# Second expert product on four 32-column tiles of TensorE at once, with rows scattered per round

## The chip, the core and the metric

The kernel runs on one core of a Trainium2 chip. The metric is the device time of one execution in microseconds (us), taken as the median over runs. The profile is of one execution; its span, 296.2 us, is what its engines and queues show, and is about 3 us shorter than the device time of the same runs.

The engines are named as in the profile: PE is TensorE, which multiplies matrices (PEld is its loading of weights, the stationary operand), DVE is VectorE, ACT is ScalarE, POOL is GpSimd, SP is the engine that only issues transfers.

## The reference, cut to what matters

An attention over 4 x 8 heads of 768 positions with 64 dimensions, in which each query attends to 6 chosen chunks of 32 keys, gives 3072 rows (tokens) of 512 numbers. These rows then go to one of 8 experts each:

```python
logits = x @ w_gate                      # 3072 x 8
expert_idx = np.argmax(logits, axis=1)   # one expert a token
gate_w = probs[np.arange(N), expert_idx]
out = np.zeros((N, D))
for e in range(8):
    tok_idx = np.where(expert_idx == e)[0]
    # the 80 tokens with the largest gate_w stay, the others give rows of zeros
    h = np.maximum(x[tok_idx] @ w1[e], 0.0)         # 80x512 @ 512x1024
    out[tok_idx] = gate_w[tok_idx, None] * (h @ w2[e])   # 80x1024 @ 1024x512
```

The change concerns the last product alone, `h @ w2[e]`, with its factor and its way to `out`.

## The kernel before

The work has two parts. The first, up to about 246 us, is the attention: 16 steps, one for each pair of heads of a batch, each with scores, softmax and values, and in between the routing of the batch that went before (which token goes to which expert, and which 80 stay). The rows of x are written to a buffer in device memory, `x_rows`, pair by pair; zeros are written to `out` early; the weights w1 and w2 of all experts are loaded during the attention, so that they lie in SBUF when the second part begins.

The end of the routing belongs to the last batch and can overlap with nothing: gates, ranks, a table. `rank_count` counts, `rank_hot` makes a one-hot matrix OHS, `table` (L750) sums the tokens' numbers and gate values by slot on PE, and `merge` puts them together with the earlier batches on DVE. The result is, for each of 80 slots (partitions) and 8 experts, the row number `idx` (L766) and the gate value `gT` (L770). `dT` holds what the row numbers are made from.

Then comes the expert stage, in which there is an order written out by hand. For an expert e:

- `gather(e)` (L958, POOL): an indirect transfer of 80 rows from `x_rows`.
- `turn(e)` (L967): four PE transposes, and an ACT copy (L970) to `xT`, two buffers.
- `up(e)` (L978): 32 matmuls of 80 columns, x @ w1, in two halves in PSUM. The ReLU of the first half is done by ACT (L985), that of the second half by DVE (L987); both write `hT`, two buffers, 8 blocks of 80 columns.
- `down(e)` (L1009): 8 matmuls, one for each 128 of the 1024 hidden dimensions. The stationary operand is 128 x 80 of `hT`, the moving one 128 x 512 of w2. The result is 80 x 512 in a PSUM bank (OB, two banks). DVE multiplies it by the gate value (L1013), POOL issues an indirect scatter of 80 rows of 2 KB (L1015) to `out`.
- `down_halves` takes the place of `down` for expert 7: the same in two halves of 256 columns (L994, L997, L999), so that the first half is scaled while the second is computed.

Each engine works through its instructions in the order in which they are written. On PE the order is turn(e+1), up(e), down(e-1): the product of expert e-1 runs while the ReLU of expert e is computed. `keep_warm(9)` (L814) gives PE nine matmuls without use ahead of turn(0), while the first gather is under way. A helper, `op`, gives each operation its waits from the names of what it reads and writes.

Instructions that write 32 partitions of PSUM occur in the attention already: `sums_lg` (L569) and `sums` (L583) put four matmuls with 32-column weights side by side, each to its own 32 partitions, and so does `rank_count` (L727).

Of the kernel before, what the change touches and what calls it, by code (L numbers as in the profile page):

```python
# [4 lines left out]
ALU = mybir.AluOpType  # L5
ACTF = mybir.ActivationFunctionType
# [3 lines left out]
U32 = mybir.dt.uint32  # L10
# [137 lines left out]
def bass_quest_chunk_select__then__topk_capacity_drop_kernel(  # L148
# [55 lines left out]
    with ExitStack() as pers:  # L204
# [3 lines left out]
        def al(stack, nm, shape, dt=F32, psum=False):  # L208
            cnt[0] += 1
            f = nc.psum_tensor if psum else nc.sbuf_tensor  # L210
            return stack.enter_context(f(nm + "_" + str(cnt[0]), list(shape), dt))
# [10 lines left out]
        with nc.Block() as blk:  # L222

            @blk.sync
            def _body(_unused):
# [68 lines left out]
                mk = al(pers, "mk", [CAP, E], U32)  # L294
                rk8 = al(pers, "rk8", [CAP, E])
                idx = al(pers, "idx", [CAP, E], U32)


                def Cs(b, jt, n, lo, w):
# [36 lines left out]
                    return bass.AP(rq, (e % 2) * 160, [[S, 128], [1, 160]]).bitcast(BF16)  # L336

                def hTv(e):
                    return bass.AP(qT[e % 2], 0, [[S, 128], [1, FB * CAP // 2]]).bitcast(BF16)

                def yv(e):
                    return bass.AP(EXB, 2048 + (e % 4) * 512, [[EXP, CAP], [1, Dm]])

                def yk(e):
                    return f"y{e % 4}"

                MBf = bass.AP(MB, 0, [[1024, 128], [1, 1024]]).bitcast(F32)
                ubm = bass.AP(M0, 192, [[512, 128], [160, 2], [32, NT - 1], [1, 32]])
# [270 lines left out]
                def scale_rows(i):  # L619
                    b, p = i // NPB, i % NPB  # L620
                    xi = bass.AP(OB, 0, [[1024, 128], [128, NT], [D, 2], [1, D]])
                    xo = bass.AP(xp, 0, [[NT * 128, 128], [128, NT], [D, 2], [1, D]])
                    rx = bass.AP(rden, 0, [[NT * 2, 128], [2, NT], [1, 2], [0, D]])
                    op("dve", lambda: ve.tensor_tensor(xo, xi, rx, ALU.mult), r=["O0", "O1", "rden"], w=["xp"])  # L624
                    xdst = bass.AP(xd.tensor, xd.offset + b * S * Dm + p * 128, [[Dm, 128], [128 * Dm, NT], [1, 128]])
                    op("sp", lambda: sp.dma_start(xdst, xp[:]), r=["xp"], w=[f"xd{i}"],
                       dsem=f"d_xd")
# [126 lines left out]
                def merge(b):  # L754
                    tv = M0[0:CAP, 0:5 * E].rearrange("p (a b) -> p a b", a=5)
                    if b == 0:
                        op("dve", lambda: ve.tensor_copy(dT[:], tv), r=["M0"], w=["dT"])
                        gsum(gT[:], dT, ["dT"], "gT")
                        return
                    nd = 2 if b == B - 1 else 5  # L760
                    gsum(gN[:], tv, ["M0"], "gN")
                    op("dve", lambda: ve.tensor_tensor(mk[:], gN[:], gT[:], ALU.is_gt), r=["gN", "gT"], w=["mk"])
                    mb = bass.AP(mk, 0, [[E, CAP], [0, nd], [1, E]])
                    op("dve", lambda: ve.copy_predicated(dT[:, 0:nd, :], mb, tv[:, 0:nd, :]), r=["mk", "M0", "dT"], w=["dT"])
                    if b == B - 1:
                        op("dve", lambda: ve.scalar_tensor_tensor(idx[:], dT[:, 0, :], 8192.0, dT[:, 1, :], ALU.subtract, ALU.subtract,  # L766
                                                                  reverse0=True), r=["dT"], w=["idx"])
                    else:
                        op("dve", lambda: ve.tensor_copy(dTb[:], dT[:]), r=["dT"], w=["dTb"])
                    op("dve", lambda: ve.copy_predicated(gT[:], mk[:], gN[:]), r=["mk", "gN", "gT"], w=["gT"])  # L770

                def sort_rows(split):
                    for e in range(E):
# [162 lines left out]
                rank_row(b)  # L936
                rank_pred()
                gate_cols(b)
                scale_rows(NP - 1)
                gate_digits(b)  # L940
                last_cmp(5)
# [5 lines left out]
                rank_count(b, (5, 4, 1, 3, 2, 0))  # L947
                rank_slot(b)
                rank_hot(b)
                table(b)  # L950
                merge(b)


                XD = [f"xd{i}" for i in range(NP)]
# [17 lines left out]
                def up(e):  # L972
                    s = e % 2
                    for hf in range(2):
                        for fb in range(hf * 4, hf * 4 + 4):
                            for d in range(DB):
                                o = SC[s][:, hf * 512 + (fb % 4) * CAP:hf * 512 + (fb % 4 + 1) * CAP]
                                op("pe", lambda: pe.matmul(o, w1s[e][:, d, ts(fb)], xTv(e)[:, d * CAP:(d + 1) * CAP],  # L978
                                                           start=(d == 0), stop=(d == DB - 1)),
                                   r=[f"w1_{e}", f"xT{s}"], w=[f"H{s}{hf}", f"SC{s}"], inc=(fb % 4 == 3 and d == DB - 1))  # L980
                        src = SC[s][:, hf * 512:hf * 512 + 4 * CAP]
                        dst = hTv(e)[:, hf * 4 * CAP:(hf + 1) * 4 * CAP]
                        k0 = [f"qT{s}"] if e < 2 and hf == 0 else []
                        if hf == 0:
                            op("act", lambda: ac.activation(dst, src, ACTF.Relu), r=[f"H{s}{hf}"], w=[f"hT{s}{hf}"] + k0)  # L985
                        else:
                            op("dve", lambda: ve.tensor_scalar(dst, src, 0.0, None, ALU.max), r=[f"H{s}{hf}"], w=[f"hT{s}{hf}"])  # L987

                def down_halves(e):
                    s = e % 2  # L990
                    for hf, o, k in ((0, OB[0:CAP, s * 512:s * 512 + Dm // 2], f"O{s}"), (1, SC[1 - s][0:CAP, 0:Dm // 2], f"SC{1 - s}")):
                        cs = slice(hf * Dm // 2, (hf + 1) * Dm // 2)
                        for fb in range(FB):
                            op("pe", lambda: pe.matmul(o, hTv(e)[:, fb * CAP:(fb + 1) * CAP], w2v(e)[:, fb, cs],  # L994
                                                       start=(fb == 0), stop=(fb == FB - 1)),
                               r=[f"hT{s}{fb // 4}"] + w2k(e), w=[k], inc=(fb == FB - 1))
                        op("dve", lambda: ve.tensor_scalar(yv(e)[:, cs], o, gT[:, e:e + 1], None, ALU.mult),  # L997
                           r=[k, "gT"], w=[yk(e)])
                    op("gpd", lambda: gp.indirect_dma_start(  # L999
                        out, bass.IndirectOffsetOnAxis(ap=idx[:, e:e + 1], axis=0), yv(e), None,  # L1000
                        bounds_check=NTOK - 1, oob_is_err=False), r=[yk(e), "idx"] + [f"outz{g}" for g in range(B)], w=[f"out{e}"], dsem=f"d_o{e % 4}")

                def down(e):
                    s = e % 2
                    if e == E - 1:
                        return down_halves(e)
                    o = OB[0:CAP, s * 512:s * 512 + Dm]
                    for fb in range(FB):
                        op("pe", lambda: pe.matmul(o, hTv(e)[:, fb * CAP:(fb + 1) * CAP], w2v(e)[:, fb, :],  # L1009
                                                   start=(fb == 0), stop=(fb == FB - 1)),  # L1010
                           r=[f"hT{s}{fb // 4}"] + w2k(e), w=[f"O{s}"], inc=(fb == FB - 1))
                    k0 = ["E2", "E3", "E4", "E5"] if e == 0 else []
                    op("dve", lambda: ve.tensor_scalar(yv(e), o, gT[:, e:e + 1], None, ALU.mult),  # L1013
                       r=[f"O{s}", "gT"], w=[yk(e)] + k0)
                    op("gpd", lambda: gp.indirect_dma_start(  # L1015
                        out, bass.IndirectOffsetOnAxis(ap=idx[:, e:e + 1], axis=0), yv(e), None,
                        bounds_check=NTOK - 1, oob_is_err=False), r=[yk(e), "idx"] + [f"outz{g}" for g in range(B)], w=[f"out{e}"], dsem=f"d_o{e % 4}")

                for e in range(3):
                    gather(e)  # L1020
                keep_warm(9)
                turn(0)
                gather(3)
# [3 lines left out]
                for e in range(1, E):  # L1027
                    if 1 < e + 1 < E:
                        turn(e + 1)
                        if e + 4 < E:  # L1030
                            gather(e + 4)
                    up(e)
                    down(e - 1)
                down(E - 1)
                sy.wait_for("sp", [f"d_o{m}" for m in range(4)])

        sy.close()
# [33 lines left out]
```

## Time and profile before

| what | value |
|---|---|
| device time, median of 3 runs | 299.59 us (299.08 to 306.82) |
| span of the profiled execution | 296.2 us |
| PE busy | 277.8 us (94%) |
| DVE, ACT, POOL busy | 208.8, 145.0, 233.8 us |
| first matmul of turn(0) | 262.89 us |
| start of up(0), up(1), down(0) | 263.74, 266.58, 268.20 us |
| last matmuls of expert 7 end at about | 290.7 us |
| last scatter begins on POOL | 292.04 us |
| matmuls of L1009 | 56, of 379 ns |
| matmuls of L994 | 16, of 272 ns |
| indirect transfers on POOL | 16, of about 0.93 us each, 2.6 us to landing |

A matmul's recorded time is from its start to the modelled end of its last result; matmuls overlap, so that the distance from one start to the next is shorter than the record. Times in the profile count from the start of the span. A "granted clock" of 1.00 is TensorE at full speed.

### The profile page before, as it was taken

The page shows a single profiled execution, that of the slowest core. Times are in us where ns is not written, and L with a number is a line of the kernel's source. Part 1 is how long each engine was busy: PE and PEld are TensorE (multiplying, and loading weights), DVE is VectorE, ACT ScalarE, POOL GpSimd, SP SyncE. Part 2 cuts the span into 40 slices and gives each one's busy share as a digit, 9 for nine tenths or more (in the row PEclk, how much of TensorE's full clock was granted, in tenths as well). Part 3 has the DMA queues.
Part 4 walks back from the last instruction along what each step waited for, and adds up shares of the span by engine and source line. Part 5 has one row for each costly group of instructions (what it writes and reads, how often), then busy time and mean ns, then how long its engine had stood idle before and what let it go on. Part 6 is the DMA issues. An engine that isn't in the chain of part 4 may idle for free.

```text
span 296.2 us, 8268 instructions
## 1 busy us (share of the span) xinstructions
PE 277.8 (94%) x3400; PEld 171.9 (58%) x3402; DVE 208.8 (70%) x561; ACT 145.0 (49%) x197; POOL 233.8 (79%) x299
## 2 busy tenths in 40 slices
PE   7679999999999999999999999999999999579992
PEld 7245565655656565656565657565646566247662
DVE  3867282746797989659889898898897886803332
ACT  2155646565657555545764546566654541512210
POOL 5049999989898999989899999898999993055332
PEclk9779999999999999999999999999999999879999
DMA  9998999998999999999999999899438299511212
GB/s 150 172 156 135 294 190 138 291 229 154 165 159 197 183 164 186 182 187 169 165 186 177 168 174 214 133 192 361 169 69 158 21 175 191 99 41 47 61 45 66
DMA packets 155141, 47.52 MB, mean 160 GB/s; under 512 B 139128, under 2 KB 147444, under 8 KB 155104
## 3 DMA queue, kind: packets, MB, share of 16 engines
q1 hardware_dynamic: 138528, 27.95, 47.9%
q0 software_dynamic: 13440, 18.67, 38.7%
q10 hardware_dynamic: 3136, 0.39, 0.9%
q8 instruction: 26, 0.43, 0.6%
q14 instruction: 11, 0.09, 0.1%
HBM read 53.10 MB, written 10.75 MB: 216 GB/s over the span
## 4 chain that ended last, share of the span: by engine, by line
PE 67%; POOL 16%; DVE 6%; DMA 6%; issue 2%; ACTq 1%; POOLq 0%; ACT 0%; DVEq 0%
PE SC L510 21%; PE OB L560 18%; POOL ES L549 12%; PE SC L525 4%; PE OB L1009 4%; DMA x_rows<-xp 4%; PE SC L978 4%; PE M L583 4%; PE OB L604 3%; POOL EXB L540 3%; PE M L473 2%; PE M L569 2%; PE MB L498 2%; DMA kn<-in_k_dram 1%; DMA qn<-x_rows,idx 1%
## 5 line engine op out<-in xcount | busy, mean ns | idle before, releaser
L530 ACT ACTIVATE EXB<-SC 128x1024 f32<-128x1024 f32 x96 | 86.2, 916 | 49.2 <-PE SC L525 47.9
L549 POOL TENSOR_TENSOR ES<-ES,EXB 128x256 f32<-128x256 f32 (+1 forms) x108 | 105.7, 991 | 4.9
L510 PE MATMUL SC<-qT,kT 64*128 64x512 f32 (+3 forms) x512 | 99.5, 479 | 1.0 <-ACT EXB L530 1.0
L560 PE MATMUL OB<-EXB,vn 128*64 128x256 f32 (+2 forms) x704 | 72.3, 360 | 0.4 <-POOL EXB L540 0.4
L560 PEld LDWEIGHTS OB<-EXB,vn 128*64 128x64 f32 x704 | 47.0, 137 | 23.6 <-issue 9.0
L510 PEld LDWEIGHTS SC<-qT,kT 64*128 64x128 f32 x512 | 42.6, 191 | 25.0 <-issue 15.1
L549 POOL TENSOR_TENSOR ES<-EXB 128x768 f32<-128x768 f32 (+1 forms) x32 | 49.9, 1558 | 2.7
L525 PE MATMUL SC<-unsT,ind 64*128 64x128 bf16 (+5 forms) x256 | 38.3, 294 | 0.8 <-ACT unsT L500 0.8
L564 ACT ACTIVATE oT<-OB 128x512 f32<-128x512 f32 (+1 forms) x32 | 15.6, 489 | 44.3 <-PE OB L560 44.3
L540 POOL TENSOR_SCALAR_AFFINE_SELECT EXB<-EXB 128x256 f32<-128x256 f32 x80 | 35.1, 448 | 0.0
L525 PEld LDWEIGHTS SC<-unsT,ind 64*128 64x128 bf16 x256 | 13.0, 96 | 18.3 <-issue 8.0
L574 DVE STREAM_TRANSPOSE M<-M 128x192 f32<-128x192 f32 x16 | 6.3, 394 | 23.1 <-PE M L583 21.2
L441 DVE STREAM_TRANSPOSE qT<-qn 128x768 f32<-128x768 f32 x16 | 15.6, 972 | 9.4 <-PE SC L525 9.4
L624 DVE TENSOR_TENSOR xp<-OB,rden 128x768 bf16<-128x768 f32 x16 | 15.3, 955 | 7.0 <-PE OB L604 6.1
L445 ACT ACTIVATE rq<-qT 128x768 f32<-128x768 f32 x16 | 13.5, 843 | 9.7 <-DVE qT L441 8.9
L451 DVE STREAM_TRANSPOSE kT<-kn 128x768 f32<-128x768 f32 x16 | 15.5, 967 | 3.6 <-DMA kn<-in_k_dram 3.5
L1015 POOL DMA_INDIRECT out_dram<-EXB,idx x7 | 6.5, 931 | 12.8 <-DVE EXB L1013 7.8
L958 POOL DMA_INDIRECT qn<-x_rows,idx x4 | 3.9, 982 | 15.7 <-DVE gT L770 13.2
L455 DVE TENSOR_REDUCE kmm<-kT 128x24 f32<-128x768 f32 x16 | 15.2, 950 | 0.5
L457 POOL TENSOR_TENSOR kmm<-kmx,kmm 128x24 f32<-128x24 f32 x16 | 7.3, 454 | 10.4 <-DVE wg L833 6.8
L456 DVE TENSOR_REDUCE kmx<-kT 128x24 f32<-128x768 f32 x16 | 15.1, 943 | 0.0
L487 DVE MAX8 top<-M 128x8 f32<-128x8 f32 (+4 forms) x160 | 14.6, 166 | 0.6
(163 smaller groups left out, 404.7 us busy)
## 6 DMA issues: line engine op xcount, KB each, us to landing
w1s<-in_moe_w_dram POOLq DMA_DIRECT2D x8, 1024.0 KB, 9.2
w2s<-in_moe_w_dram POOLq DMA_DIRECT2D x7, 1024.0 KB, 10.6
qn<-in_q_dram SPq DMA_DIRECT2D x64, 96.0 KB, 3.3
vn<-in_v_dram SPq DMA_DIRECT2D x32, 192.0 KB, 3.5
out_dram<-w1s SPq DMA_DIRECT2D x4, 1536.0 KB, 9.1
kn<-in_k_dram SPq DMA_DIRECT2D x60, 96.0 KB, 3.2
x_rows<-xp SPq DMA_DIRECT2D x16, 192.0 KB, 4.7
EXB<-in_moe_w_dram POOLq DMA_DIRECT2D x1, 1024.0 KB, 10.8
```

The costliest lines, as they stand in the source:

```text
L441: op("dve", lambda: ve.transpose(qT[j][:], qn[s][:].rearrange("p a b c -> p (a b c)")), r=[f"qn{s}{g}" for g in range(4)], w=[f"qT{j}"])
L451: op("dve", lambda: ve.transpose(kT[j][:], kn[s][:].rearrange("p a b c -> p (a b c)")), r=[f"kn{s}{g}" for g in range(4)], w=[f"kT{j}"])
L455: op("dve", lambda: ve.tensor_reduce(kmm[j][:, 0, 0:NCH], kv, AX, ALU.min), r=[f"kT{j}"], w=[f"kmm{j}"])
L456: op("dve", lambda: ve.tensor_reduce(kmx[:], kv, AX, ALU.max), r=[f"kT{j}"], w=["kmx"])
L510: op("pe", lambda: pe.matmul(o, kT[j][pr, ts(kt)], qT[j][pr, q0:q1], start=True, stop=False), r=[f"kT{j}", f"qT{j}"], w=[f"SC{s}"], inc=False)
L525: op("pe", lambda: pe.matmul(o, ind[pr, ts(kt)], unsT[j][pr, b0 - 128:q1 - 128], start=False, stop=True), r=[f"ind{h}", f"unsT{j}"], w=[f" ...
L530: op("act", lambda: ac.activation(Ex(st, None, 0, W), src, ACTF.Exp, scale=SCALE), r=[f"SC{s}"], w=[f"E{st}"])
L540: op("gp", lambda: gp.affine_select(ad, a, pattern=[[0, 2], [1, 128]], compare_op=ALU.is_ge, fill=0.0, base=0, channel_multiplier=-1), r=[ ...
L549: op("gp", lambda: gp.tensor_tensor(o, in0, in1, ALU.add), r=[f"E{s2}", f"E{first[0]}"] if first else [f"E{s2}"] + kt, w=kt)
L560: op("pe", lambda: pe.matmul(OB[pr, q0:q1], vn[s][:, kt, h, :], ex, start=(n == 0), stop=last), r=[f"vn{s}{h}", "ES0" if st is None else f ...
L564: op("act", lambda: ac.activation(oT[:, q0:q1], OB[:, q0:q1], ACTF.Copy), r=[f"O{bk}"], w=[f"oT{bk}"])
L624: op("dve", lambda: ve.tensor_tensor(xo, xi, rx, ALU.mult), r=["O0", "O1", "rden"], w=["xp"])
```

## The change

The 80 slots of an expert become groups of 32, 32 and 16, padded to 32: 96 columns. Twelve such groups, those of four experts, fit in three rounds of four. In a round the four groups take the four 32-column tiles of the array, each with its own weights from `hT` and its own moving operand from its expert's w2. There are six rounds in place of eight products.

```diff
+ROUNDS = [[(0, 0), (0, 1), (0, 2), (1, 0)], [(1, 1), (1, 2), (2, 0), (2, 1)], [(2, 2), (3, 0), (3, 1), (3, 2)]]
...
-                    o = OB[0:CAP, s * 512:s * 512 + Dm]
-                    for fb in range(FB):
-                        op("pe", lambda: pe.matmul(o, hTv(e)[:, fb * CAP:(fb + 1) * CAP], w2v(e)[:, fb, :],
-                                                   start=(fb == 0), stop=(fb == FB - 1)),
-                           r=[f"hT{s}{fb // 4}"] + w2k(e), w=[f"O{s}"], inc=(fb == FB - 1))
...
+                        for fb in range(FB):
+                            for g, (e, sb) in enumerate(groups):
+                                op("pe", lambda: pe.matmul(o[g * 32:g * 32 + 32, :], hTv(e)[:, fb * HW + sb * 32:fb * HW + sb * 32 + 32],
+                                                           w2v(e)[:, fb, c0:c1], start=(fb == 0), stop=(fb == FB - 1)),
+                                   r=[f"hT{e % 4}{fb // 4}"] + w2k(e), w=[k], inc=(fb == FB - 1 and g == 3))
...
+                        op("dve", lambda: ve.tensor_scalar(yv(r)[:, c0:c1], o, gR[:, r:r + 1], None, ALU.mult),
```

What goes with it:

- `hT` gets four buffers of 8 x 96 columns (in the place of qT and kT of the attention, free by then), and four memsets on DVE clear the 16 padding columns; they stand after `gate_cols(b)`, ahead of `scale_rows`.
- The row numbers and gate values, which lie by slot and expert, are needed by partition of the round. A new function `spread` does this with twelve small matmuls on PE (each picks 32 slots of one expert with 32 columns of the identity; 6 columns wide) and three DVE operations, which give `idR` and `gR`, 128 x 6. It stands after gather(0) to gather(2) and ahead of keep_warm(9).
- So that one table holds both, the gate values are copied to `dT[:, 2, :]` by DVE after `rank_hot`, and the last `copy_predicated` of `merge` goes there.
- A scatter moves the rows of a round, 128 partitions, of which 96 or 112 hold tokens; padding gets row number 8192, which lies past the end and is left out.
- The last round is computed in two halves of 256 columns, as expert 7 was.

The order on PE becomes, with d for a round:

```diff
-                for e in range(1, E):
...
-                    up(e)
-                    down(e - 1)
-                down(E - 1)
+                    up(e)
+                    if e % 4 > 0 and e != 3:
+                        down(e // 4 * 3 + e % 4 - 1)
+                    elif e == 4:
+                        down(2)
```

that is up0, up1 d0, up2 d1, up3, up4 d2, up5 d3, up6 d4, up7 d5, each up with the turn of the next expert ahead of it. Rounds 0, 1, 3, 4 and 5 use the expert whose up stands just ahead of them; before, another up or another down lay between.

More of the change, by code (lines that the diff above doesn't have):

```diff
@@ L296, in _body @@
                 idx = al(pers, "idx", [CAP, E], U32)
+                gR = al(pers, "gR", [128, 6])
+                idR = al(pers, "idR", [128, 6], U32)
                 def Cs(b, jt, n, lo, w):
@@ L338, in hTv, with yv @@
                 def hTv(e):
[L339 to L345, printed above, removed]
+                    return bass.AP((qT, kT)[e // 2 % 2][e % 2], 0, [[S, 128], [1, FB * HW // 2]]).bitcast(BF16)
+                def yv(r):
+                    return bass.AP(EXB, 2048 + (r % 4) * 512, [[EXP, 128], [1, Dm]])
+                HW = 96
+                ROUNDS = [[(0, 0), (0, 1), (0, 2), (1, 0)], [(1, 1), (1, 2), (2, 0), (2, 1)], [(2, 2), (3, 0), (3, 1), (3, 2)]]
                 MBf = bass.AP(MB, 0, [[1024, 128], [1, 1024]]).bitcast(F32)
@@ L769, in merge @@
                         op("dve", lambda: ve.tensor_copy(dTb[:], dT[:]), r=["dT"], w=["dTb"])
-                    op("dve", lambda: ve.copy_predicated(gT[:], mk[:], gN[:]), r=["mk", "gN", "gT"], w=["gT"])
+                    if b == B - 1:
+                        op("dve", lambda: ve.copy_predicated(dT[:, 2, :], mk[:], gN[:]), r=["mk", "gN", "dT"], w=["dT"])
+                    else:
+                        op("dve", lambda: ve.copy_predicated(gT[:], mk[:], gN[:]), r=["mk", "gN", "gT"], w=["gT"])
                 def sort_rows(split):
@@ L938, in _body @@
                 gate_cols(b)
+                for e in range(4):
+                    t = (qT, kT)[e // 2 % 2][e % 2]
+                    op("dve", lambda: ve.memset(bass.AP(t, CAP // 2, [[S, 128], [HW // 2, FB], [1, (HW - CAP) // 2]]), 0.0), w=[("qT", "kT")[e // 2] + str(e % 2)])
                 scale_rows(NP - 1)
@@ L949, in _body, with spread @@
                 rank_hot(b)
+                op("dve", lambda: ve.tensor_copy(dT[:, 2, :], gT[:]), r=["gT", "dT"], w=["dT"])
                 table(b)
                 merge(b)
+                def spread():
+                    for r, groups in enumerate(ROUNDS):
+                        for g, (e, sb) in enumerate(groups):
+                            tq = bass.AP(dT, e, [[5 * E, CAP], [4, 2], [E, 3]])
+                            op("pe", lambda: pe.matmul(M0[g * 32:g * 32 + 32, r * 6:r * 6 + 6], ident_f[0:CAP, sb * 32:sb * 32 + 32], tq,
+                                                       start=True, stop=True),
+                               r=["dT", "ident_f"], w=["M0"], inc=(r == 2 and g == 3))
+                    mv = M0[:, 0:18].rearrange("p (r q v) -> p q r v", r=3, q=2)
+                    o6 = bass.AP(gR, 0, [[6, 128], [3, 2], [1, 3]])
+                    i6 = bass.AP(idR, 0, [[6, 128], [3, 2], [1, 3]])
+                    op("dve", lambda: ve.tensor_copy(o6, mv[:, :, :, 0]), r=["M0"], w=["gR"])
+                    op("dve", lambda: ve.scalar_tensor_tensor(i6, o6, 8192.0, mv[:, :, :, 1], ALU.subtract, ALU.subtract,
+                                                              reverse0=True), r=["M0", "gR"], w=["idR"])
+                    op("dve", lambda: ve.tensor_copy(o6, mv[:, :, :, 2]), r=["M0", "idR"], w=["gR"])
                 XD = [f"xd{i}" for i in range(NP)]
@@ L980, in up @@
                                    r=[f"w1_{e}", f"xT{s}"], w=[f"H{s}{hf}", f"SC{s}"], inc=(fb % 4 == 3 and d == DB - 1))
-                        src = SC[s][:, hf * 512:hf * 512 + 4 * CAP]
-                        dst = hTv(e)[:, hf * 4 * CAP:(hf + 1) * 4 * CAP]
-                        k0 = [f"qT{s}"] if e < 2 and hf == 0 else []
+                        src = SC[s][:, hf * 512:hf * 512 + 4 * CAP].rearrange('p (f c) -> p f c', f=4)
+                        dst = hTv(e)[:, hf * 4 * HW:(hf + 1) * 4 * HW].rearrange('p (f c) -> p f c', f=4)[:, :, 0:CAP]
@@ L984, in up @@
+                        k0 = [("qT", "kT")[e // 2] + str(s)] if e < 4 and hf == 0 else []
                         if hf == 0:
-                            op("act", lambda: ac.activation(dst, src, ACTF.Relu), r=[f"H{s}{hf}"], w=[f"hT{s}{hf}"] + k0)
+                            op("act", lambda: ac.activation(dst, src, ACTF.Relu), r=[f"H{s}{hf}"], w=[f"hT{e % 4}{hf}"] + k0)
                         else:
-                            op("dve", lambda: ve.tensor_scalar(dst, src, 0.0, None, ALU.max), r=[f"H{s}{hf}"], w=[f"hT{s}{hf}"])
@@ L989, in down_halves @@
[L989 to L992, printed above, removed]
-                        for fb in range(FB):
-                            op("pe", lambda: pe.matmul(o, hTv(e)[:, fb * CAP:(fb + 1) * CAP], w2v(e)[:, fb, cs],
-                                                       start=(fb == 0), stop=(fb == FB - 1)),
-                               r=[f"hT{s}{fb // 4}"] + w2k(e), w=[k], inc=(fb == FB - 1))
-                        op("dve", lambda: ve.tensor_scalar(yv(e)[:, cs], o, gT[:, e:e + 1], None, ALU.mult),
-                           r=[k, "gT"], w=[yk(e)])
-                    op("gpd", lambda: gp.indirect_dma_start(
-                        out, bass.IndirectOffsetOnAxis(ap=idx[:, e:e + 1], axis=0), yv(e), None,
-                        bounds_check=NTOK - 1, oob_is_err=False), r=[yk(e), "idx"] + [f"outz{g}" for g in range(B)], w=[f"out{e}"], dsem=f"d_o{e % 4}")
@@ L1003, in down @@
[L1003 to L1006, printed above, removed]
-                    o = OB[0:CAP, s * 512:s * 512 + Dm]
-                    for fb in range(FB):
-                        op("pe", lambda: pe.matmul(o, hTv(e)[:, fb * CAP:(fb + 1) * CAP], w2v(e)[:, fb, :],
-                                                   start=(fb == 0), stop=(fb == FB - 1)),
-                           r=[f"hT{s}{fb // 4}"] + w2k(e), w=[f"O{s}"], inc=(fb == FB - 1))
[L1012 to L1017, printed above, removed]
+                            op("dve", lambda: ve.tensor_scalar(dst, src, 0.0, None, ALU.max), r=[f"H{s}{hf}"], w=[f"hT{e % 4}{hf}"])
@@ new lines, in down @@
+                def down(r):
+                    last = r == 5
+                    groups = [(r // 3 * 4 + e, sb) for e, sb in ROUNDS[r % 3]]
+                    o = OB[:, r % 2 * 512:r % 2 * 512 + Dm]
+                    parts = [(o, f"O{r % 2}", 0, Dm)]
+                    if last:
+                        n = Dm // 2
+                        parts = [(o[:, 0:n], f"O{r % 2}", 0, n), (SC[0][:, 0:n], "SC0", n, Dm)]
+                    for o, k, c0, c1 in parts:
+                        for fb in range(FB):
+                            for g, (e, sb) in enumerate(groups):
+                                op("pe", lambda: pe.matmul(o[g * 32:g * 32 + 32, :], hTv(e)[:, fb * HW + sb * 32:fb * HW + sb * 32 + 32],
+                                                           w2v(e)[:, fb, c0:c1], start=(fb == 0), stop=(fb == FB - 1)),
+                                   r=[f"hT{e % 4}{fb // 4}"] + w2k(e), w=[k], inc=(fb == FB - 1 and g == 3))
+                        k0 = ["E2", "E3", "E4", "E5"] if r == 0 else []
+                        op("dve", lambda: ve.tensor_scalar(yv(r)[:, c0:c1], o, gR[:, r:r + 1], None, ALU.mult),
+                           r=[k, "gR"], w=[f"y{r % 4}"] + k0)
+                    op("gpd", lambda: gp.indirect_dma_start(
+                        out, bass.IndirectOffsetOnAxis(ap=idR[:, r:r + 1], axis=0), yv(r), None,
+                        bounds_check=NTOK - 1, oob_is_err=False), r=[f"y{r % 4}", "idR"] + [f"outz{g}" for g in range(B)], w=[f"out{r}"], dsem=f"d_o{r % 4}")
@@ L1019, in _body @@
                 for e in range(3):
                     gather(e)
+                spread()
                 keep_warm(9)
```

## The prediction

> **What bounds the kernel now.** I read the chain that ended last first, because only what lies on it can shorten the time. Up to 246 us it runs through the attention, which the change leaves alone. From 263.7 us on it is PE almost without a gap (columns: start, us on the path, engine, tile, line):
>
> ```profile
> 260.22 2.63 DMA qn<-x_rows,idx
> 263.25 0.45 ACT rq L970
> 263.74 1.96 PE SC L978 x32
> 266.09 0.45 ACT rq L970
> 266.58 1.78 PE SC L978 x32
> 268.36 1.73 PE OB L1009 x8
> 270.24 1.15 PE SC L978 x32
> 271.39 1.73 PE OB L1009 x8
> ...
> 276.28 0.50 PE SC L978 x14
> 277.65 0.60 PE SC L978 x12
> 278.25 1.73 PE OB L1009 x8
> ...
> 287.17 1.73 PE OB L1009 x8
> 288.90 0.89 PE OB L994 x8
> 289.81 0.49 DVE EXB L997
> 290.49 0.81 POOL out_dram L1015
> ```
>
> The reader is to see that the second product is on the path with 1.73 us an expert, that it alternates with the first product, and that the tail is DVE and then POOL. So PE time saved in `down` is time saved, as long as nothing else comes to the front. Between 276.5 and 277.65 us there is one hole of about 0.7 us in which PE waited for nothing that the profile shows ("issue").
>
> The second view is the timeline of PE in the attention, where matmuls with 32-column weights stand between full-width ones (start, us from the first start to the last end, count last):
>
> ```profile
> 233.09 0.35 PE L525 MATMUL SC<-unsT,ind 64*128 64x448 bf16 x2
> 233.37 0.16 PEld L569 LDWEIGHTS M<-oT,wg 128*32 128x32 f32 x8 [0.61 <-issue]
> 233.37 0.53 PE L569 MATMUL M<-oT,wg 128*32 128x192 f32 x8
> ...
> 233.72 0.85 PE L583 MATMUL M<-ES,onc 128*32 128x192 f32 x16
> 234.50 0.30 PEld L510 LDWEIGHTS SC<-qT,kT 64*128 64x128 f32 x4 [0.30 <-issue]
> 234.50 1.13 PE L510 MATMUL SC<-qT,kT 64*128 64x512 f32 x4
> ```
>
> From the start times at full clock, a matmul of L1009 (379 ns long) follows the one before after 1.73/8 = 0.216 us; the other 0.163 us is a tail that overlaps. A record of L583 lasts 326 ns, so it occupies its columns 0.326 - 0.163 = 0.163 us. Sixteen in a row would take 16 x 0.163 = 2.6 us; they took 0.85 - 0.163 = 0.69 us. That is 3.8 at once, with weights loaded for each. It is the best evidence that the profile has for the new form.
>
> The third view is the table of stretches, for the granted clock around `keep_warm` (columns: stretch, length, busy time and count of PE, PEld, DVE, ACT, POOL, then clock):
>
> ```profile
> 259.50:260.00 0.50, 0.50 (x3) 0.21 (x2) 0.00 (x0) 0.00 (x0) 0.00 (x0) 0.50 0.00 0
> 261.00:261.50 0.50, 0.50 (x3) 0.10 (x1) 0.00 (x0) 0.00 (x0) 0.27 (x1) 1.00 0.00 0
> 265.00:265.50 0.50, 0.50 (x12) 0.50 (x9) 0.00 (x0) 0.32 (x1) 0.42 (x1) 0.50 0.02 4
> 268.00:268.50 0.50, 0.50 (x13) 0.40 (x10) 0.00 (x0) 0.26 (x1) 0.26 (x1) 1.00 0.00 0
> ```
>
> The clock was half from 257.3 to 260.7 us, full to 264.2, half to 267.5, then full. Up(0) and up(1) ran mostly at half clock: 1.96 and 1.78 us as against 1.15 on the path later (about 1.3 from first start to last end).
>
> **What the Trainium skill says.** "TensorEngine Tiling (Array Packing)", Key Properties: tiles load weights and multiply in parallel, but a change of tiling mode drains the engine. The trace agrees with both. The drain can be read above: the second L525 began at 233.09 or just after and would have let the next start after 0.187 us (448 columns at the 0.42 ns a column of L1009), at 233.28; L569 began at 233.37, 0.09 later. On the way back, the last L583 ends at 234.57, its columns are free 0.163 earlier, at 234.41, and L510 starts at 234.50, again 0.09. "TensorE: Matmul & The Clock Gate", Part 3, gives 2.38 times for three column tiles of 512 columns in one pack; the trace's sustained run is closer to ideal. The same page, Part 1, says that the clock falls to half after an idle window of about 3.4 us that runs freely, and rises after a busy one; the trace's changes at 257.3, 260.7, 264.2 and 267.5 are 3.4 apart, so it agrees.
>
> **The change part by part.**
>
> 1. Two products fewer. Eight products of 1.73 us become six rounds; a round streams 8 times 512 columns through each of four tiles at once, 8 x 0.216 = 1.73 us if all four overlap. Saved on the path: 2 x 1.73 = **-3.46**. The last one is in halves before and after, with the same 1.73.
>
> 2. Overlap that is not perfect. L583 lost 0.69 - 0.65 = 0.04 us over a run of sixteen, which is the staggered start. As a fixed loss it is 6 x 0.04 = 0.24, as a share (5% of 1.73) 6 x 0.09 = 0.54. I take **+0.3**.
>
> 3. Mode changes. Each round needs one into 32-column tiles and all but the last one out: 11 x 0.1 = **+1.1**. Nothing hides this, PE is the path.
>
> 4. Rounds that use the up just ahead. In the steady pattern up starts at 282.98, ACT's ReLU of its first half (L985) runs from 283.76 to 284.20, and L1009 starts at 284.13. A mode change puts the start at 284.23, and ACT to PE takes 0.05 (266.53 to 266.58), so PE is released at 284.25. In each of the five rounds the first one to three groups of a pass are of an older expert and need not wait. The second half's ReLU (DVE, 284.33 to 284.82) is needed at the fifth pass, 4 x 0.216 = 0.86 after the start: hidden. **+0.1** in all. Queued behind a waiting matmul is all later PE work, so this would be paid in full.
>
> 5. Four memsets on DVE: an analogous 128x64 memset takes 112 ns, four with their spacing about 0.55. DVE idles 0.39 just there, ahead of `scale_rows` (L624), waiting for the store of x_rows before it. The rest, **+0.15**, is on the path: L624, the comparisons and the table follow on DVE without a gap.
>
> 6. The copy of gate values, about 0.19 (L804), lies in the 0.48 that DVE waits for the table (L750): 0. `copy_predicated` only changes its target, behind `idx`, for which the gather waits: 0. The three DVE operations of `spread` run while DVE has nothing to do till 266: 0. DVE scales six times in place of eight, and turns and gathers stay: 0, since gather(6) and gather(7) still land about 3 us ahead of their turns behind the earlier scatters.
>
> 7. `spread` on PE and what it pushes. It must wait for DVE until 259.33; before, keep_warm had started at 258.2. Twelve f32 matmuls give 24 records; 15 to 30 ns each gives 0.36 to 0.7, and a mode change 0.1. keep_warm then starts at about 260.1, 1.9 later. Nine matmuls last 3.84 at half clock (0.427 each, the spacing in the trace), 1.95 at full. At half clock they end at 264.0 and delay turn(0), which before began at 262.89, by 1.1. Yet PE is then busy up to turn(0) and beyond, so up(0) and up(1) run at full clock and win back about (1.96-1.3) + (1.78-1.3) = 1.1. If the clock rises in the middle, the delay is small and the gain comes nearly whole. From -1.0 to +0.9; I take **0**.
>
> 8. The scatter. POOL's 0.93 for 80 rows may be fixed or go with the rows: 0.93 to 0.93 x 128/80 = 1.49. Only the last is on the path (it began 0.81 after its DVE operation ended at 291.23, and that delay stays); it also moves 96 rows instead of 80. Bounds 0 to +0.7; I take **+0.3**.
>
> 9. Instructions. PE gets 224 down matmuls for 72 and 12 more, each with a weight load, so it fetches more. The hole at 276.5 may be a late fetch; a second one would cost +0.7. Taken as 0.
>
> Sum: -3.46 + 0.3 + 1.1 + 0.1 + 0.15 + 0 + 0.3 = -1.5. 299.6 - 1.5 = **298.1 us**.
>
> **The rivals.**
>
> - *The clock pays too.* Point 7 at -1.0, drains half hidden (-0.5) and a fixed POOL cost (-0.3): -3.3, 296.3 us. For it: PE is busy from keep_warm through turn(0). Against it: the windows run freely, and keep_warm may fall in the cold one whole.
> - *Given back at both ends.* keep_warm in the way (+0.9), a second instruction hole (+0.7), the scatter at its upper bound (+0.4): -1.5 + 2.0 = +0.5, 300.1 us, slower than before. For it: keep_warm really starts behind a wait now. Against it: all three must come together.
> - *The tiles do not stream four at once with 512 bf16 columns of four separate sources.* At two at once a round takes 3.46, six take 20.8 as against 13.8: +7.0, with the rest +1.95, 308.5 us. Against it: L583 at 3.8, with f32 sources, twice the bytes an element, at 0.85 ns a column.
>
> **How the numbers follow.** Forecast 0.53, clock pays 0.20, given back 0.21, tiles do not overlap 0.06. The range spans the two middle rivals with a few tenths: 295.9 to 300.7. More than 2% (6 us) faster needs 293.6, which no case reaches: 0.02. Slower by 2% (305.6) is the last rival: 0.06. Within 2%: 0.92.
>
> **What would show it.** A round's 32 matmuls should last 1.9 to 2.0 us from first start to last end, and the turn or up behind it start some 0.1 later than the spacing asks. Up(0) and up(1) should take nearer 1.3 than 1.9 and keep_warm end after 262.5. The last matmul to the end of the span, 5.5 us before, should grow by no more than 0.7. A round above 2.3 us, or a PE wait of more than 0.2 for ReLU in each round, would prove me wrong, as would a gather that PE waits for beyond the first.

## The result and the profile after

The changed kernel is a little faster. Against the kernel before it gave a ratio of **0.9886** (95% interval 0.9856 to 0.9917), which is 3.4 us of 299.3. Two later measurements of the same file, with more runs, gave 0.9963 (0.9941 to 0.9986) and 0.9967 (0.9914 to 1.002), about 1 us. The first ratio rests on two executions of the changed kernel, the later ones on 17 and 7. So the gain is 1 to 3.4 us, the lower end being better supported, and the last interval just reaches no gain at all; 1.5 had been forecast. The medians over all runs of the first measurement, 299.04 against 299.33 us, lie closer together because they contain disturbed runs (above 301 us), which the ratios leave out.

The two profiled executions differ by 1.9 us: the span went from 296.2 to 294.3. First the chain that ended last, in the changed kernel (start, us on the path, engine, tile, line; L1025 is the second product, L1003 the first, L995 the ACT copy of a turn, L1029 the scaling by DVE):

```profile
265.23 2.53 DMA kn<-x_rows,idx
267.84 0.44 ACT rq L995
268.66 1.90 PE OB L1025 x29
270.81 1.15 PE SC L1003 x32
271.96 1.88 PE OB L1025 x32
273.86 0.76 DVE EXB L1029
274.67 0.55 issue
275.44 1.01 POOL out_dram L1031
276.76 2.57 DMA kn<-x_rows,idx
279.41 0.44 ACT rq L995
280.23 1.90 PE OB L1025 x29
282.38 1.15 PE SC L1003 x32
283.53 1.85 PE OB L1025 x32
285.39 1.25 PE SC L1003 x32
286.64 1.20 PE OB L1025 x32
287.84 0.90 PE SC L1025 x32
288.83 0.50 DVE EXB L1029
```

Six rounds of about 1.9 us stand where eight products of 1.73 stood. New is that the chain leaves PE twice, before round 0 and before round 3: it goes through a gather (DMA) and an ACT copy, and then 29 of the 32 matmuls of the round follow. The second of these gathers is itself late because POOL issues it behind the scatter of round 1 (275.44). The timeline of the changed kernel at round 0 says what happened (start, us from first start to last end, engine, line; in brackets the idle time before and what ended it):

```profile
266.69 1.32 PE L1003 MATMUL SC<-rq,w1s 128*128 128x80 bf16 x32 [0.39 <-ACT rq L995]
...
267.84 0.44 ACT L995 ACTIVATE rq<-MB 128x320 bf16<-128x320 bf16 x1 [1.20 <-DMA kn<-x_rows,idx]
267.94 0.40 PE L1025 MATMUL OB<-w2s,qT 128*32 128x512 bf16 x3
...
268.17 0.43 ACT L1010 ACTIVATE qT<-SC 128x320 bf16<-128x320 f32 x1
268.66 1.90 PE L1025 MATMUL OB<-w2s,qT 128*32 128x512 bf16 x29 [0.32 <-ACT qT L1010]
```

The three groups of expert 0 start at 267.94. The fourth group is of expert 1 and needs the ReLU of its first half (L1010). That ReLU stands in ACT's queue behind the copy of turn(2), and the copy waits until gather(3) has landed. A gather does not write or read the copy's target, xT; it is only listed as a reader of it, so as to be issued after an earlier copy. That listing also makes the next copy to the same buffer wait for the gather. PE loses 268.66 - 267.94 - 0.02 = 0.7 us, where 0.02 is by how much a fourth tile starts later anyway. Round 3 shows the same with gather(7): its first three matmuls start at 279.68, the fourth at 280.23, a loss of 0.5 us.

A round without that wait, with what follows it, in the same timeline:

```profile
276.44 1.91 PE L1025 MATMUL OB<-w2s,kT 128*32 128x512 bf16 x32
...
278.28 0.32 PE L992 MATMUL MB<-ident_bf,qn 80*128 80x80 bf16 x4
```

1.91 us from the first start to the last end, less the tail of 0.163, is 1.75 for 32 matmuls of 0.216, or 8 times 0.216: four ran at once. The next transpose starts 0.07 before the recorded end instead of 0.163, so the change of tiling mode costs 0.09.

And the granted clock, in the table of stretches of the changed kernel (stretch, length, busy time and count of PE, PEld, DVE, ACT, POOL, then the clock):

```profile
261.00:261.50 0.50, 0.50 (x3) 0.22 (x2) 0.00 (x0) 0.00 (x0) 0.19 (x2) 0.50 0.00 0
...
264.50:265.00 0.50, 0.50 (x9) 0.50 (x10) 0.00 (x0) 0.00 (x0) 0.00 (x0) 0.53 0.33 90
265.00:265.50 0.50, 0.50 (x19) 0.50 (x17) 0.00 (x0) 0.02 (x1) 0.27 (x1) 1.00 0.00 0
```

keep_warm ran at half clock to its end (263.71). up(0) began at half and was at full clock after half a microsecond (1.51 us from first start to last end), and up(1) ran at full (1.32 us). Before, the clock rose within keep_warm and was back at half for most of up(0) and up(1) (1.96 and 1.78 us). So turn(0) starts 0.6 us later, at 263.50, and the two ups win that back.

### The profile page after: what moved, and what is told of

It is laid out like the page before. It is cut to its first block, busy times and chain, and to the rows that moved or that the text cites. A ratio compares the mean times of both kernels' runs of the same rounds, so it can differ in the third digit from the quotient of the medians.

```text
span 294.3 us, 8617 instructions
## 1 busy us (share of the span) xinstructions
PE 274.5 (93%) x3576; PEld 168.7 (57%) x3578; DVE 208.3 (71%) x567; ACT 144.8 (49%) x197; POOL 232.4 (79%) x297
## 4 chain that ended last, share of the span: by engine, by line
PE 60%; POOL 23%; DVE 7%; issue 3%; DMA 3%; ACT 1%; ACTq 1%; POOLq 0%; DVEq 0%
PE SC L513 18%; PE OB L563 18%; POOL ES L552 16%; POOL EXB L543 4%; PE SC L528 4%; PE M L586 3%; PE OB L1025 3%; PE OB L607 3%; PE M L476 2%; PE M L572 2%; DMA kn<-x_rows,idx 2%; DMA kn<-in_k_dram 1%; PE MB L501 1%; PE SC L820 1%; PE SC L1003 1%
## 5 line engine op out<-in xcount | busy, mean ns | idle before, releaser
L513 PE MATMUL SC<-qT,kT 64*128 64x512 f32 (+3 forms) x512 | 97.4, 471 | 1.0 <-ACT EXB L533 1.0
L513 PEld LDWEIGHTS SC<-qT,kT 64*128 64x128 f32 x512 | 41.6, 187 | 24.1 <-issue 14.2
L627 DVE TENSOR_TENSOR xp<-OB,rden 128x768 bf16<-128x768 f32 x16 | 15.3, 955 | 6.6 <-PE OB L607 6.1
L1031 POOL DMA_INDIRECT out_dram<-EXB,idR x6 | 6.0, 994 | 12.5 <-DVE EXB L1029 11.6
```

The source lines that it names most:

```text
L513: op("pe", lambda: pe.matmul(o, kT[j][pr, ts(kt)], qT[j][pr, q0:q1], start=True, stop=False), r=[f"kT{j}", f"qT{j}"], w=[f"SC{s}"], inc=False)
```

## The experiments

Two theories stood at the start. **Theory A**: two products fewer on PE pay, mode changes and ReLU waits give part of it back. **Theory B**: the gain comes from the clock, since `spread` moves the warm-up up to turn(0). Ratios are to the kernel before, with 95% intervals. Line numbers shift by a few between kernels.

### The change again

No edit.

> The changed kernel as it is, beside the kernel before and the variants below. Theory A (PE columns): two products fewer save 3.5 us, eleven mode changes of 0.1 us and two ReLU waits of about 0.6 us give back 2.2, and the rest moves by a few tenths: 2 to 3.5 us faster than before (ratio 0.988 to 0.993). Theory B (clock: the gain is that spread moves the warm-up matmuls up to turn(0)): the same total, so this run does not tell them apart; it gives the number that the variants are compared with.

Measured: 0.9963 (0.9941 to 0.9986). Its trace has the wait for gather(7) again, longer than in the first trace: in round 3 PE loses 1.2 us between the third matmul and the fourth.

```profile
280.78 0.40 PE L1025 MATMUL OB<-w2s,qT 128*32 128x512 bf16 x3
...
281.97 1.90 PE L1025 MATMUL OB<-w2s,qT 128*32 128x512 bf16 x29 [0.79 <-ACT qT L1010]
```

### spread alone, in the kernel before

```diff
+                spread()
                 keep_warm(9)
```

> The kernel before with the twelve small matmuls of spread and its three DVE operations in the place that they have in the changed kernel, their outputs unused, and everything else as before. Theory A: the warm-up matmuls start 1.5 us later, turn(0) begins about 0.6 later, up(0) and up(1) run faster: -0.5 to +0.3 us against before. Theory B: most of the 2 to 3.4 us of gain shows here already, -1.5 us or more.

Measured: **0.9999** (0.9974 to 1.0024). In its trace turn(0) begins at 263.55 and up(0) takes 1.59 us as against 1.96 before; what is lost ahead is won behind. Theory B expected a gain of 1.5 us or more (a ratio of 0.995 or less) here, which the interval excludes, so it falls.

### spread behind the warm-up, in the changed kernel

```diff
-                spread()
                 keep_warm(9)
+                spread()
```

> The changed kernel with spread behind the nine warm-up matmuls instead of ahead of them, so that they start 1.9 us earlier as in the kernel before, and spread runs in the gap in which PE waits for the first gather. Theory B (clock): the gain goes back, up(0) and up(1) at half clock again, 0.5 to 1 us slower than the change. Theory A: turn(0) begins 0.6 us earlier and up(0), up(1) lose as much, within 0.5 us of the change.

Measured: 0.9952 (0.9905 to 0.9999), not to be told from the change. In its trace up(0) ran at half clock (2.31 us), and no loss against the change shows in the time. The interval is too wide to exclude the 0.5 to 1 us that theory B expected, so this run alone decides nothing.

### The two loops of a round exchanged

```diff
-                        for fb in range(FB):
-                            for g, (e, sb) in enumerate(groups):
+                        for g, (e, sb) in enumerate(groups):
+                            for fb in range(FB):
```

> The changed kernel with the two loops of a round exchanged: all eight matmuls of one group follow each other on one 32-column tile before the next group begins on the next tile. Same matmuls, same number. Theory A (what saves is that four tiles stream at once, and PE takes its matmuls in order, so neighbours must be on different tiles): a round takes nearly 32 x 0.216 = 6.9 us in place of 1.9, 6 x 5 = 30 us slower, about 325 us. The rival (the tiles overlap in whatever order the matmuls are given, or the gain has another source): within 3 us of the changed kernel.

Measured: 310.24 us, a single run. The timeline and the chain of this kernel show a round each:

```profile
268.25 4.54 PE L1025 MATMUL OB<-w2s,qT 128*32 128x512 bf16 x32
```

```profile
274.18 4.47 PE OB L1025 x32
```

So the gain hangs on the order: the same 32 matmuls take 4.54 us instead of 1.91, and the kernel becomes some 12 us slower than the change. But they do not take the 6.9 us of 32 matmuls one after the other. 4.54 - 0.163 = 4.38 us is 20.3 times 0.216. In round 1 the first matmul of the third tile starts 1.76 us after the first of the first tile, 8 times 0.216: each tile starts four matmuls after the one before it, and 8 + 3 x 4 = 20. The description ahead of the prediction has each engine work in the order written. For the starts of PE's matmuls this does not hold here: the third tile's first matmul (kT) starts ahead of one of the second tile (qT) that stands before it in the program.

```profile
275.87 0.39 PE L1025 MATMUL OB<-w2s,kT 128*32 128x512 bf16 x1
276.08 0.38 PE L1025 MATMUL OB<-w2s,qT 128*32 128x512 bf16 x1
```

The starts look as if PE took on about four matmuls for a busy tile before those behind them had to wait; that is inferred from these starts and was not tested. Both expectations were off; A's direction was right, its size was not.

### Gathers issued freely

```diff
-                        r=XD + ["idx"] + ([f"xT{(e - 3) % 2}"] if e > 2 else []), w=[xgk(e)], dsem=f"d_g{e}")
+                        r=XD + ["idx"], w=[xgk(e)], dsem=f"d_g{e}")
```

> The changed kernel, but the gathers of experts 3 to 7 no longer count as readers of xT, so that they are issued without waiting for the ACT copy of an earlier turn, and the copy of turn(2) and turn(6) does not wait for gather(3) and gather(7) to land. Theory A says that this wait holds up ACT and through it the ReLU of experts 1 and 5, which down(0) and down(3) need at once: PE's stalls of 0.6 and 0.5 us in rounds 0 and 3 go, 0.8 to 1.2 us faster than the changed kernel. The rival (PE would have waited anyway, for the gathers or for the ReLU itself): no change, 0 to 0.3 us.

Measured: **1.0044** (1.0019 to 1.0068), 0.8% or 2.4 us slower than the change beside it (0.9963). Neither theory foresaw that. The edit does two things: it frees the copy, and it lets six gathers follow each other on POOL. The next two runs take these apart, though on another chip.

### Only the copy freed

The gathers keep their place; only the copy's wait for their landing goes.

```diff
                        bounds_check=NTOK - 1, oob_is_err=False),
                        r=XD + ["idx"] + ([f"xT{(e - 3) % 2}"] if e > 2 else []), w=[xgk(e)], dsem=f"d_g{e}")
+                    if e > 2:
+                        sy.lr[f"xT{(e - 3) % 2}"].pop(f"d_g{e}")
```

> The changed kernel with one wait less: the gathers of experts 3 to 7 are issued where they were (each still waits for the ACT copy three turns earlier), but the copy of a later turn to the same xT buffer no longer waits for that gather to land, as a gather doesn't touch xT. Theory A: ACT's ReLU of experts 1 and 5 comes on time, the stalls of 0.6 and 0.5 us in rounds 0 and 3 go, ratio to before about 0.992 to 0.994 (0.8 to 1.2 us less than the change). Rival (gathers under way hold PE's results up, whoever waits for them, which made the freely issued gathers slower): no better than the change, 0.996 or above.

Measured: **0.9904** (0.9875 to 0.9933), median 294.94 us against 299.01. That is 0.6% below the run of the change above, though taken on another chip and at another time. The chain of this kernel (L1027 is the second product, L1005 the first):

```profile
265.88 1.32 PE SC L1005 x32
267.21 1.85 PE OB L1027 x32
269.31 1.15 PE SC L1005 x32
270.46 1.86 PE OB L1027 x32
...
277.10 1.15 PE SC L1005 x32
278.25 1.85 PE OB L1027 x32
```

Rounds 0 and 3 now have all their 32 matmuls in a row, and no gather stands on the path. From the start of up(0) to the last scatter it is 24.2 us (263.89 to 288.08) as against 25.6 in the first trace of the change (264.50 to 290.11). Of the 1.4 us less, 1.2 are the two waits (0.7 and 0.5) and 0.2 the clock, which was at full for all of up(0) here (1.32 us instead of 1.51). It is the version to keep: the interval lies wholly below the kernel before, and the wait is gone. That it is faster than the change is shown by the trace and not yet by times, since the two were not measured side by side; the run with `spread` behind the warm-up, taken beside it and keeping the wait, has an interval that overlaps (0.9905 to 0.9999).

The repetition was to be beside the change:

> The changed kernel with the ACT copy no longer waiting for a gather to land, again, now beside the change itself. Theory A (the wait holds up ReLUs that the rounds need at once): 0.8 to 2 us less than the change. Rival (the two calls of before fell on different chips or hours, and the copies are equal): within 0.5 us of the change.

It gave too few runs for a ratio, and stays inconclusive. In its trace round 3 has all its matmuls in a row, but round 0 takes 2.41 us: DVE's ReLU of up(1) starts 0.75 us after the recorded end of up(1). More on such delays below.

### No late gathers at all

```diff
                 def gather(e):
+                    if e > 2:
+                        return
...
-                        op("pe", lambda: pe.transpose(tp[:, d * CAP:(d + 1) * CAP], xgv(e)[:, ts(d)], ident_bf[0:CAP, 0:CAP]),
+                        op("pe", lambda: pe.transpose(tp[:, d * CAP:(d + 1) * CAP], xgv(e % 3)[:, ts(d)], ident_bf[0:CAP, 0:CAP]),
```

> The changed kernel without the gathers of experts 3 to 7; their turns read the rows of experts 0 to 2 instead, so that the operands stay real numbers and the outputs of experts 3 to 7 are not the reference's. Rival (gathers hold up PE's results): the late starts of the ReLUs after the end of PE's matmuls (0.7 to 3 us in other runs) are gone, and the time falls by 2 us or more below the change, ratio 0.989 or less. Theory A without it: only the two ACT stalls go, ratio about 0.992 to 0.994.

Measured: 0.9896 (0.9864 to 0.9928), the same as with the copy freed; the kernel leaves out five gathers, so its rows for experts 3 to 7 are not those of the reference. In their place and with the copy free, gathers 3 to 7 cost nothing beyond these intervals (0.3%). The freely issued ones also have the copy free, and differ only in how close the gathers follow each other. They are 0.8% slower than the change beside them, and 1.4% slower than this pair on the other chip; so following close seems to cost time, but what in it does was not found.

### The copy freed in the kernel before

The same two lines, in the kernel before.

> The kernel before with the same wait removed and nothing else. Theory A: the wait is there before as well, but a product runs on PE between a ReLU and its use, so nothing is gained: 0 to -0.4 us, ratio 0.998 to 1.001. Rival (the wait costs about the same in both kernels and has nothing to do with the change): 1 to 2 us less, ratio 0.996 or below.

Measured: 1.0009 (0.9953 to 1.0066). Nothing is gained, as theory A expects, but the interval just reaches the rival's bound. The trace before has the same wait, in the copy of turn(2):

```profile
267.10 0.44 ACT L970 ACTIVATE rq<-MB 128x320 bf16<-128x320 bf16 x1 [0.57 <-DMA kn<-x_rows,idx]
```

Behind it PE runs the product of expert 0, which is ready.

### Rounds grouped

The copy freed, and three rounds behind four ups:

```diff
-                    if e % 4 > 0 and e != 3:
-                        down(e // 4 * 3 + e % 4 - 1)
-                    elif e == 4:
-                        down(2)
+                    if e % 4 == 3:
+                        for r in range(3):
+                            down(e // 4 * 3 + r)
```

> As the run in which the copy is not held, and with the rounds of four experts one behind the other: up 0 to 3, rounds 0 to 2, up 4 to 7, rounds 3 to 5. Three mode changes in place of eleven, and no round but the first and fourth stands right behind the ReLU that it needs. If a mode change costs 0.1 us, 0.8 us less than with the copy not held; against that turn(3) and turn(4) come 3 us earlier and may wait for their gathers, up to 1.5 us. Ratio to before 0.988 to 0.997; the trace should show L1025 from round to round without the gap of 0.1.

Measured: 0.9907 (0.9876 to 0.9938), no better than without grouping. From its chain:

```profile
267.68 2.51 DMA qn<-x_rows,idx
270.55 1.15 PE SC L1005 x32
271.70 5.29 PE OB L1027 x96
```

Three rounds in a row take 5.29 us, 1.76 each, as against 1.85 to 1.9 alone, so the mode changes do fall away. But turn(4), which stands ahead of up(3) on PE, now waits for gather(4): PE could have taken it up at 269.63 (the start of up(2), 268.48, plus 1.15), and it starts at 270.23. That is 0.6 us of the 0.8 that eight mode changes fewer save.

With the copy freed and only the second set grouped:

> The changed kernel with the copy not held, and with rounds 3 to 5 one behind the other after up 4 to 7; rounds 0 to 2 stay where they were, as grouping them made turn(4) wait for its gather. Six mode changes less cost 0.1 us each less than with the copy not held alone if they cost what the gaps in the traces say: 0.4 to 0.9 us less, ratio about 0.987 to 0.989. Rival (PE has the time anyway, the scatters at the end, now closer together on POOL, set the end): no change or 0.3 us more.

Measured: 0.9934 (0.9888 to 0.998). The change itself was run beside it on the same chip:

> The changed kernel once more, on the same chip and beside the same runs of the kernel before as the three that follow, so that they can be compared directly. Two measurements gave 0.9886 and 0.9963; expected 0.989 to 0.997.

Measured: 0.9967 (0.9914 to 1.002). The intervals overlap almost wholly, and the two kernels differ in the freed copy as well, so whether grouping there pays stays open.

## Why the prediction was right

The time fell within the range, the mechanism of the main term was right, and the sum was of the right size. But two terms, points 4 and 9, were wrong by about a microsecond each and in opposite directions, so that the total came out well is in part luck. In the profiled pair, by the prediction's own points:

| point | forecast | in the profiled pair |
|---|---|---|
| 1 two products fewer | -3.46 | -3.46: rounds stream four at once |
| 2 imperfect overlap | +0.3 | +0.1: the fourth tile starts 0.01 to 0.03 after the first |
| 3 eleven mode changes | +1.1 | +1.1: 0.09 to 0.10 each |
| 4 ReLU waits | +0.1 | **+1.4**: 0.7, 0.5 and 0.2 |
| 5 memsets | +0.15 | 0: done in the gap, L627 starts at 250.76, before 250.81 |
| 7 spread and clock | 0 | -0.36: down(0) starts 0.26 earlier (267.94 for 268.20), though a mode change (0.1, point 3) now lies ahead of it |
| 8 scatter | +0.3 | 0: 0.97 instead of 0.91 on POOL, and 5.0 from the end of the last scaling to the end, as before |
| 9 hole in PE | 0 | **-0.8**: it is gone |
| sum | -1.5 | -2.0 (the last scatter begins 1.93 earlier) |

The **mis-sized term is point 4**. I took the timing of the ReLU from the steady pattern late in the stage, where ACT is free. In rounds 0 and 3 ACT is held by a copy that waits for a gather. The trace before has that wait too (267.10, shown above), but nothing depended on it there. Point 6 looked at the gathers only ahead of their own turns, where gather(7) does land 2.7 us early (279.33 for 282.06), and not at the copy that also waits for it. The run with the copy freed, whose rounds 0 and 3 have no such wait, supports this. The smaller part, 0.2, is in the last round: with 256 columns the fifth pass comes 0.43 us after the start, not 0.86, and three of its four groups wait for DVE's half (they start at 287.22 instead of 287.04).

Two signs that the prediction had named as proving it wrong did appear: a round above 2.3 us (round 0 took 2.62 and round 3 took 2.45, with their waits), and gathers beyond the first that hold PE up, here by way of ACT.

That this loss did not show in the total is due to point 9. Point 9 left the hole as it was or allowed a second one; that the change might remove it was not considered. In the trace before PE stops twice within up(4), for 0.8 us in all, and DVE starts the ReLU of up(3) 2.5 us after the recorded end of up(3), 274.41:

```profile
276.12 1.13 PE L978 MATMUL SC<-rq,w1s 128*128 128x80 bf16 x20
276.93 0.49 DVE L987 TENSOR_SCALAR qT<-SC 128x320 bf16<-128x320 f32 x1 [3.03 <-PE M L967]
277.65 0.60 PE L978 MATMUL SC<-rq,w1s 128*128 128x80 bf16 x12 [0.40 <-issue]
```

It recurs. The two other traces of the kernel before, with `spread` alone and with the copy freed, have a stop in the same up(4), of 1.0 and 0.5 us:

```profile
278.01 0.63 PE L998 MATMUL SC<-rq,w1s 128*128 128x80 bf16 x13 [0.54 <-issue]
```

```profile
279.29 0.30 PE L980 MATMUL SC<-rq,w1s 128*128 128x80 bf16 x4 [0.33 <-issue]
```

None of the eleven traces of the changed kernel and its variants has one there: up(4) takes 1.11 or 1.12 us from the first start to the last start in each, as against 1.93, 2.15 and 1.61. Six of the eleven come from the same two chips as the two other traces of the kernel before. So its absence seems to belong to what the change gains. What causes the hole, and why the change removes it, was not found; no run tested it.

PE's results also reach the other engines late elsewhere. In the trace of the change run again, PE's up(0) ends by the record at 266.21, but DVE's ReLU of its second half starts only at 266.95.

```profile
264.89 1.32 PE L1003 MATMUL SC<-rq,w1s 128*128 128x80 bf16 x32 [0.53 <-ACT rq L995]
...
266.95 0.49 DVE L1012 TENSOR_SCALAR qT<-SC 128x320 bf16<-128x320 f32 x1 [5.51 <-PE MB L992]
```

In the change's first trace this step took 0.05 (266.01 to 266.06). A delay of 0.5 us or more after up(0) or up(1) stands in the trace before and in all eight that were taken on two of the chips. It stands in none of the four taken on a third chip, to which the runs with the copy freed, without late gathers and with rounds grouped belong, nor in the change's first trace. It may go with the chip; its cause was not found. The late gathers, issued in their place, are not shown to be the cause: the run without them is no faster than the one with the copy freed. In the change run again the delay cost about 0.6 us (1.46 instead of 0.84 from turn(1) to up(1)). Of the 1.8 us by which its span is longer than in the first trace, 1.0 had arisen before the expert stage (`table` starts at 258.65 instead of 257.67), so these delays are one part among several of the spread between 1 and 3.4 us of gain.

Of the rivals, "the clock pays too" falls with the run of `spread` alone, though its fixed cost on POOL came true; "the tiles do not stream four at once" falls with the 1.91 us of a round; and "given back at both ends" found neither a delay at down(0), nor a second hole, nor a dearer scatter.

## What to carry to other kernels

Column tiles with separate moving operands ran four at once when neighbours in the instruction stream were on different tiles (1.91 us a round, as against 4.54 in the other order), so put the tile loop inside. Count what each switch to and from full width took here, 0.09 to 0.10 us. A schedule that brings a producer next to its consumer makes every earlier wait in the producer's queue count: look in the trace before for waits that cost nothing there, on the engine that makes the operand. And an ordering that is expressed as a read also binds the next writer: express only the half that is meant.

## What the runs showed of the hardware

- With groups in turn on the tiles, each tile started four matmuls after the one before, not eight: 4.54 us a round, neither 1.9 nor 6.9.
- With the tiles written one after the other, PE started matmuls of a later tile (275.87) ahead of earlier-written ones of a busy tile (276.08).
- A change between 128-column and 32-column tiles took 0.09 to 0.10 us.
- The indirect scatter of 128 partitions, 96 to 112 of them with rows, took POOL 0.97 to 1.03 us, that of 80 rows 0.91 to 0.96: nearly fixed.
- Results of PE sometimes reached the waiting engine well after their recorded end: 0.74 us in one trace of the changed kernel, 0.05 at the same place in another. All eight traces from two chips had delays of 0.5 us or more after up(0) or up(1), none of the four from a third.
- PE stopped within up(4) for 0.5 to 1.0 us in three of three traces of the kernel before, and in none of eleven of the changed kernel and its variants; the cause stays open.
